# Reads of repeated a and b over all SBUF ports, v in six DMAs, and another order of the first interleaved batch, in a polysketch attention with a sinkhorn-routed MoE behind it

## The chip, the core and the metric

The kernel runs on one core of a Trainium2 chip. The metric is the device time of one execution in microseconds. TensorE (PE) does the matrix products, VectorE (DVE) and ScalarE (ACT) the elementwise work, GpSimd (POOL) some sums and weights, and SyncE (SP) issues nearly all DMA transfers. On-chip memory (SBUF) has 128 partitions; PSUM is the memory into which TensorE writes. All data are float32.

## The reference

Sizes: B = 4 batches, H = 4 heads, S = 1088 positions, D = 32 per head, r = 8 sketch rows; then N = 4352 tokens of 128 numbers, E = 8 experts of F = 1024 hidden units.

```
def phi(x):                                   # 64 features from two sketches of 8
    a = einsum('rd,bhsd->bhsr', S1, x)
    b = einsum('rd,bhsd->bhsr', S2, x)
    return einsum('bhsi,bhsj->bhsij', a, b).reshape(..., 64)
kv  = einsum('bhsf,bhsd->bhfd', phi(k), v);   z = sum(phi(k), axis=2)
num = einsum('bhsf,bhfd->bhsd', phi(q), kv)
den = einsum('bhsf,bhf->bhs', phi(q), z)[..., None] + 1e-06
x   = (num / den) transposed to (B*S, H*D) = (4352, 128)

P = exp(x @ w_gate - max)                     # 4352 x 8
for _ in range(8):
    P /= P.sum(1, keepdims=True) + 1e-09;  P /= P.sum(0, keepdims=True) + 1e-09;  P *= N / E
out = sum over e of P[:, e:e+1] * (relu(x @ w1[e]) @ w2[e])
```

So every token goes through every expert, and P is only a weight. That is why experts 0 and 1 can be computed before P is known (their results are weighted later), and why the big products can start while most of the attention is still to be done.

## The kernel before

**The big products.** Nearly all TensorE time is in the MoE: `first` (L895) multiplies w1 by columns of x into a PSUM bank, ScalarE applies relu (L899), VectorE forms sums and differences of blocks (L912 for the form with seven products, L957 for that with twenty), and `second`/`into` (L1068) multiplies w2, or sums of its blocks, by these into the banks s. The generator `steps()` yields one step of this at a time: one first product and the second products that fall due, 8 steps behind (`LAG`). `fill(n)` takes steps from it until n units are done; a unit is 480 columns. The first groups of columns belong to experts 0 and 1 without weights: 2 x 256 and 2 x 288 columns of batch 0 for expert 0, 2 x 256 for expert 1, then three times 2 x 480 and 2 x 192 columns of batches 1 to 3. After routing, weighted columns xe = xT * P (L664 on GpSimd) of the other experts follow to the end.

**The attention.** Batch 0 is written out by hand at the start, before any step of the MoE can run; its last third, `multiply(2)`, `fractions(2)`, `divide(2)`, falls after the first `fill`. Batches 1 to 3 are interleaved with the MoE. Their parts:

- `transpose_k` (L293, VectorE) turns k, `keys_ab` (L299, TensorE, matmuls at L306 and L310) makes the two sketches of the keys, `keys_products` (VectorE) their outer products, `keys_sums` (L328, TensorE) kv and z together, with a slot of ones beside the heads' slots of v giving z; `keys_kept` (L344) copies the result from PSUM to kvs.
- `transpose_q` (L290) turns q; `queries_ab` (L417, matmuls at L426) makes the sketches a and b of the queries, ScalarE copies them from PSUM to the tile qab, and SyncE writes them to DRAM (qa, qb). Some are written several times over: the outer product of a and b needs each a beside each b on 64 partitions per pair of heads.
- `repeat` (L438) reads them back repeated: rb from qb in two DMAs of 64 partitions, and ph from qa in eight DMAs, each to the partitions j, j+8, j+16 and so on.
- `times` (L449) multiplies ph by rb on VectorE, a third of the positions at a time; `tops` (L453, TensorE, L460) multiplies by kvs; `over` (L470, VectorE) divides; `take_over` (L481) writes the turned result to DRAM (xd) and reads it into xT in four DMAs. From xT the MoE takes its columns.

`attention(b)` (L497) strings these together with the next batch's keys and queries in between: at its first points come `keys_sums(b)`, `times(b,0)`, `transpose_q(b+1)`, then `keys_kept(b)`, `queries_ab(b+1)`, `times(b,1)`, `tops(b,0)`, then `times(b,2)`, `repeat(b+1)`, `over(b,0)`, `tops(b,1)`. Between any two points 1.4 units of MoE work are filled in. `routing` follows with 5 units before its first product and 3.75 per iteration of P; then its result goes through DRAM (pT) to the weighted columns.

**What sets the order.** In these stretches the order of instructions on TensorE and VectorE is that of the program text (`tc.manual_schedule`), so a waiting instruction holds up everything behind it on its engine. ScalarE's relus and the DMA issues on SyncE's one queue are placed by the scheduler, in practice close to the order of the text. Four PSUM banks serve all first products and the small products of attention in turn (`bank()`).

**Buffers.** ph has two buffers (one batch each, by turns), rb, qT, kT, qab, kp have one, v two, q two, k one. So `repeat(b+1)` can read rb only when the last `times(b,2)` is done, and `load_k(b+2)` can start only when `transpose_k(b+1)` is done.

## Time and profile before

Device time: 950.99 us, the median of 3 runs (949.77 to 951.51). The profiled execution has a span of 949.6 us.

| stretch of the span, us | TensorE busy, us | granted TensorE clock | DMA share | what happens |
|---|---|---|---|---|
| 0 to 20 | 16.92 | 1.00 | 0.63 | batch 0 of attention by hand, with 15 products at the start that only keep TensorE busy |
| 20 to 50 | 19.18 | 0.87 | 0.80 | end of batch 0, keys and queries of batch 1, first MoE steps |
| 50 to 110 | 55.52 | 0.95 | 0.80 | batches 1 to 3 between MoE steps |
| 110 to 200 | 86.64 | 0.98 | 0.10 | plain experts 0 and 1; the end of attention and routing |
| 200 to 215 | 15.00 | 1.00 | 0.27 | the first weighted columns are made |
| 215 to 950 | 726.81 | 1.00 | 0.44 | weighted experts |

The sizes of the transfers in question, and their median time from issue to landing: qb from qab 576 KB, 5.7 us (two a batch); qa from qab 72 KB, 5.7 us (two); rb from qb 576 KB, 5.6 us (two); ph from qa 144 KB, 7.5 us (eight); k and q 544 KB, 5.6 and 7.1 us; v 64 KB, 3.3 us (eight a batch) and 8 KB, 3.1 us (four).

How to read it: "busy" is the time in which an engine executes, without its waits. The granted clock is the share of full speed that TensorE was given[...]. The DMA share is the mean busy share of the core's 16 DMA engines. A line such as "PE a L426 <- DVE qT L291" in a view of waits says that TensorE's instruction at line 426, which writes tile a, waited for VectorE's instruction at line 291 that writes qT. In the chain of the end, each line is a start time, a duration and what ran or was waited for, and "DMA rb<-qb" is a transfer into rb from qb.

### The profile page before, as it was taken

What the parts mean: (1) busy time and instruction counts of PE and PEld (TensorE: products, weight loads), DVE (VectorE), ACT (ScalarE), POOL (GpSimd) and SP (SyncE); (2) the same over time, 40 slices, a digit from 0 to 9 for tenths busy, and PEclk for the clock granted to TensorE, in tenths of its full rate; (3) what the DMA queues carried; (4) which work ended last, traced back from release to release, by engine and by line L of the source; (5) the groups of instructions that cost most, each with busy time, mean ns of one, the idle gap of its engine ahead of it and who ended that gap; (6) DMA issues with size and microseconds to landing.
All of it is one profiled execution on the core that took longest, in us unless ns stands there. A gap on an engine that the chain in (4) does not pass through costs nothing.

```text
span 949.6 us, 18935 instructions
## 1 busy us (share of the span) xinstructions
PE 920.1 (97%) x7434; PEld 554.6 (58%) x7434; DVE 692.8 (73%) x1204; ACT 417.8 (44%) x905; POOL 195.3 (21%) x182
## 2 busy tenths in 40 slices
PE   8789899999999999999999999999999999999997
PEld 5567544556666666665555555555555555556964
DVE  7479669878678779567786665976666977778655
ACT  2334344555444445444544444544444544445443
POOL 2010000026357611031010200120111333320210
PEclk9889999999999999999999999999999999999999
DMA  5977610023243354553544353445343455552640
GB/s 168 234 198 199 150 47 1 1 85 128 95 139 123 106 191 138 155 177 107 163 128 147 124 166 113 145 122 167 128 145 109 148 189 175 161 186 89 170 148 12
DMA packets 93928, 127.70 MB, mean 134 GB/s; under 512 B 25904, under 2 KB 71984, under 8 KB 89488
## 3 DMA queue, kind: packets, MB, share of 16 engines
q1 hardware_dynamic: 92608, 126.34, 43.8%
q8 instruction: 58, 0.95, 0.4%
q10 hardware_dynamic: 1232, 0.16, 0.1%
q14 instruction: 30, 0.25, 0.1%
HBM read 107.88 MB, written 18.60 MB: 133 GB/s over the span
## 4 chain that ended last, share of the span: by engine, by line
PE 86%; DVE 6%; DMA 5%; issue 1%; ACT 1%; SPq 1%; POOL 0%; DVEq 0%; ACTq 0%
PE a L895 45%; PE s L1068 39%; DMA rb<-qb 2%; DMA qx<-in_q_dram 1%; DVE hb L912 1%; DMA w<-in_moe_w_dram 1%; DMA qb<-qab 1%; PE a L460 1%; DVE hb L957 1%; DMA xd<-xt 0%; PE a L426 0%; DVE pqg L957 0%; PE a L337 0%; DVE kept L721 0%; DVE cs L594 0%
## 5 line engine op out<-in xcount | busy, mean ns | idle before, releaser
L895 PE MATMUL a<-xe,w 128*64 128x256 f32 (+1 forms) x2560 | 518.2, 470 | 0.0
L899 ACT ACTIVATE hb<-a 128x256 f32<-128x256 f32 (+5 forms) x408 | 195.2, 480 | 260.5 <-PE a L895 235.1
L899 ACT ACTIVATE hx<-a 128x256 f32<-128x256 f32 (+1 forms) x360 | 167.4, 465 | 214.2 <-PE a L895 193.0
L895 PEld LDWEIGHTS a<-xe,w 128*64 128x64 f32 x2560 | 207.7, 137 | 79.3 <-issue 2.2
L1068 PE MATMUL s<-hb,ws 128*64 128x256 f32 (+4 forms) x1344 | 239.1, 395 | 2.1 <-DVE hb L912 1.6
L1068 PE MATMUL s<-hx,ws 128*64 128x256 f32 x1280 | 204.8, 379 | 0.4 <-DVE kept L724 0.4
L957 DVE TENSOR_TENSOR hx<-hx 128x512 f32<-128x512 f32 (+1 forms) x204 | 151.7, 753 | 70.1 <-ACT hx L899 65.0
L957 DVE TENSOR_TENSOR hb<-hb 128x512 f32<-128x512 f32 (+1 forms) x204 | 133.4, 665 | 94.3 <-ACT hb L899 90.3
L664 POOL TENSOR_TENSOR xe<-xT,xe 128x768 f32<-128x768 f32 (+2 forms) x41 | 84.1, 2053 | 563.7 <-DMA xe<-pT 545.8
L1068 PEld LDWEIGHTS s<-hb,ws 128*64 128x64 f32 x1344 | 113.9, 137 | 111.5 <-issue 82.3
L1068 PEld LDWEIGHTS s<-hx,ws 128*64 128x64 f32 x1280 | 106.3, 137 | 98.6 <-issue 74.3
L895 PE MATMUL a<-xT,w 128*64 128x480 f32 (+4 forms) x512 | 123.0, 475 | 1.0 <-DVE xT L410 0.9
L1068 PE MATMUL s<-hb,w 128*64 128x256 f32 (+4 forms) x496 | 102.1, 412 | 1.8 <-DVE kept L724 1.8
L912 DVE TENSOR_TENSOR hb<-hb 128x480 f32<-128x480 f32 (+8 forms) x96 | 64.5, 673 | 20.6 <-ACT hb L899 11.0
L1068 PE MATMUL s<-hx,w 128*64 128x256 f32 x384 | 68.3, 379 | 0.0
L895 PEld LDWEIGHTS a<-xT,w 128*64 128x64 f32 x512 | 51.3, 141 | 28.3 <-issue 17.6
L241 POOL TENSOR_TENSOR ws<-w 128x256 f32<-128x256 f32 (+1 forms) x70 | 59.8, 890 | 14.1 <-PE a L895 10.6
L1068 PEld LDWEIGHTS s<-hb,w 128*64 128x64 f32 x496 | 45.4, 138 | 27.9 <-issue 10.9
L912 DVE TENSOR_TENSOR hx<-hx 128x256 f32<-128x256 f32 (+1 forms) x65 | 38.7, 600 | 25.0 <-ACT hx L899 23.9
L957 DVE TENSOR_TENSOR pqg<-hb 128x512 f32<-128x512 f32 x68 | 48.3, 750 | 0.0
L1068 PEld LDWEIGHTS s<-hx,w 128*64 128x64 f32 x384 | 34.2, 137 | 10.6 <-DVE hx L912 0.3
L957 DVE TENSOR_TENSOR pqg<-hx 128x512 f32<-128x512 f32 x68 | 35.8, 566 | 0.0
(164 smaller groups left out, 468.9 us busy)
## 6 DMA issues: line engine op xcount, KB each, us to landing
w<-in_moe_w_dram SPq DMA_DIRECT2D x82, 512.0 KB, 5.4
ws<-ws SPq DMA_DIRECT2D x34, 1024.0 KB, 5.0
xe<-pT SPq DMA_DIRECT2D x34, 384.0 KB, 4.3
ws<-ws SPq DMA_DIRECT2D x12, 512.0 KB, 4.4
qb<-qab SPq DMA_DIRECT2D x6, 576.0 KB, 5.7
rb<-qb SPq DMA_DIRECT2D x6, 576.0 KB, 5.6
ph<-qa SPq DMA_DIRECT2D x24, 144.0 KB, 7.5
pb<-pT SPq DMA_DIRECT2D x6, 384.0 KB, 7.4
```

What stands on the lines that cost most here:

```text
L241: tc.keep_in_program_order(nc.gpsimd.tensor_tensor(ws[:, c:c + len(ns)], blocks(x), blocks(y), op=Alu.subtract if off else Alu.add))
L460: nc.tensor.matmul(pn[64 * s:64 * (s + 1), t, 2 * i:2 * i + 2].rearrange("p h d -> p (h d)"), ph[:, i, s, 64 * t:64 * (t + 1)], kvs[b % 2] ...
L664: tc.keep_in_program_order(nc.gpsimd.tensor_tensor(out, x, pb, op=Alu.mult))
L895: nc.tensor.matmul(ph[sl], loaded_w[j][0][:, P * f + H2 * s:P * f + H2 * (s + 1)], sources[j][:, lo:hi], start=True, stop=True, tile_posit ...
L899: nc.scalar.activation(out=out, in_=ph, func=Act.Relu)
L912: nc.vector.tensor_tensor(out, a, b, op=Alu.subtract)
L957: nc.vector.tensor_tensor(out if not isinstance(out, tuple) else places(*out), places(*a), places(*b) if isinstance(b, tuple) else b, op=A ...
L1068: nc.tensor.matmul(sums[g][i][H2 * s:H2 * (s + 1), n * place:n * (place + 1)], w, x, start=c == 1, stop=c == per, tile_position=(0, H2 * s))
```

## The change

It has four parts. First, the way in which a and b of the queries are stored in DRAM and read back. a is now stored twice (one write of 144 KB per half instead of 72 KB), so that ph can be read in four DMAs of 288 KB, each to the partitions j, j+4, j+8 and so on. b is stored by parity of the head in the pair, in four writes of 288 KB, so that rb can be read in one DMA over all 128 partitions. [...] `repeat` is split into `repeat_a`, which stands directly behind the writes in `attention`, and `repeat_b`, which stays where `repeat` was because rb has one buffer; the writes of a now go ahead of those of b.

Second, v is loaded for all four heads at once, in six DMAs per batch for twelve. For that the slot of ones moves from the middle of the tile v to its end, the slots that `keys_sums` multiplies follow, and `keys_kept` and `fractions` use the changed order of kv and z; `keys_kept` is one copy per engine instead of two.

Third, the order of batch 1's beginning: `multiply(2)` and `fractions(2)` of batch 0 come ahead of `transpose_q(1)`, and the loads of k, q and v of batch 2 stand behind `transpose_k(1)`, ahead of `keys_ab(1)`.

Fourth, more MoE steps stand between these parts: 11 units from the first `fill` to `attention(1)`, where there were 8.5.

```
--- before.py
+++ after.py
@@ -151,7 +151,7 @@
     v_slots = []
     for i in range(2):
         t = wk.tile([P, H + 1, NT + 1, D], F32, name=f"v{i}", bufs=1)
-        nc.vector.memset(t[:, 2], 1.0)
+        nc.vector.memset(t[:, H], 1.0)
         v_slots.append(t)
 
     loaded, pools = {}, []
@@ -167,18 +167,15 @@
         loaded["q", b] = qx
 
     def load_v(b):
-        vx = v_slots[b % 2]
-        for p in range(2):
-            o = v[b, 2 * p].offset
-            slots = slice(3 * p, 3 * p + 2)
-            for c in range(4):
-                nc.sync.dma_start(
-                    out=vx[32 * c:32 * (c + 1), slots, 0:NT, :].rearrange("p h t d -> p h (t d)"),
-                    in_=AP(tensor=v.tensor, offset=o + NT * D * c, ap=[[SA * D, 32], [S * D, 2], [1, NT * D]]))
-            for c in range(2):
-                nc.sync.dma_start(
-                    out=vx[32 * c:32 * (c + 1), slots, NT, :],
-                    in_=AP(tensor=v.tensor, offset=o + (4 * NT + c) * D, ap=[[SA * D, 32], [S * D, 2], [1, D]]))
+        vx, o = v_slots[b % 2], v[b].offset
+        for c in range(4):
+            nc.sync.dma_start(
+                out=vx[32 * c:32 * (c + 1), 0:H, 0:NT, :].rearrange("p h t d -> p h (t d)"),
+                in_=AP(tensor=v.tensor, offset=o + NT * D * c, ap=[[SA * D, 32], [S * D, H], [1, NT * D]]))
+        for c in range(2):
+            nc.sync.dma_start(
+                out=vx[32 * c:32 * (c + 1), 0:H, NT, :],
+                in_=AP(tensor=v.tensor, offset=o + (4 * NT + c) * D, ap=[[SA * D, 32], [S * D, H], [1, D]]))
 
     load_k(0)
     load_q(0)
@@ -328,7 +325,8 @@
 
         kp, vx = products.pop(b), v_slots[b % 2]
         pv = bank()[:, 0:128].rearrange("p (i c d) -> p i c d", i=2, c=2)
-        slots = (slice(0, 3, 2), slice(1, 3), slice(2, 4), slice(2, 5, 2))
+
+        slots = [slice(h, H + 1, H - h) for h in range(H)]
 
         for t in range(NT + 1):
             n = P if t < NT else 64
@@ -343,22 +341,16 @@
 
     def keys_kept(b):
         pv = sums_of.pop(b)
-
-        f = pv.rearrange("p i c d -> p (i c d)")
         for s in range(2):
             sl = slice(64 * s, 64 * (s + 1))
-            for i in range(2):
-                if not b:
-                    x, y = kvz[sl, :, i, s, :], pv[sl, i]
-                elif i:
-                    x, y = kvs[b % 2][sl, :, s, D], f[sl, 2 * D - 1:2 * D + 1]
-                else:
-                    x = kvs[b % 2][sl, :, s, 0:D]
-                    y = AP(tensor=f.tensor, offset=f[sl].offset, ap=[f[sl].ap[0], [3 * D, 2], [1, D]])
-                if s:
-                    nc.vector.tensor_copy(x, y)
-                else:
-                    nc.scalar.copy(x, y)
+            if b:
+                x, y = kvs[b % 2][sl, :, s, :], pv[sl].rearrange("p i c d -> p i (c d)")[:, :, 0:D + 1]
+            else:
+                x, y = kvz[sl, :, :, s, :], pv[sl].rearrange("p i c d -> p c i d")
+            if s:
+                nc.vector.tensor_copy(x, y)
+            else:
+                nc.scalar.copy(x, y)
 
     chunks = ((0, 384), (384, 736), (736, S))
 
@@ -388,7 +380,7 @@
         pn, pd = bank(), bank()
         for t, m in ((pd, 1), (pn, 0)):
             for i in range(2):
-                nc.tensor.matmul(t[64 * i:64 * (i + 1), 0:n], kvz[:, (i + m) % 2, i].rearrange("p h d -> p (h d)"),
+                nc.tensor.matmul(t[64 * i:64 * (i + 1), 0:n], kvz[:, m, i].rearrange("p h d -> p (h d)"),
                                  phs[0][:, i, lo:hi], start=True, stop=True, tile_position=(0, 64 * i))
         queries[0, c] = pn, pd
 
@@ -415,8 +407,8 @@
 
 
     def queries_ab(b):
-        qa = dram.tile([H * R, 2, 2 * W9], F32, name=f"qa{b}")
-        qb = dram.tile([R, R * H, 2, 2 * W9], F32, name=f"qb{b}")
+        qa = dram.tile([H * R, 2, 2, 2 * W9], F32, name=f"qa{b}")
+        qb = dram.tile([2, R, 2 * R, 2, 2 * W9], F32, name=f"qb{b}")
         ab = wk.tile([P, 3, 192], F32, tag="qab", name="qab", bufs=1)
         x = qT.rearrange("p (h q c t s) -> p h c t q s", h=2, q=2, c=3, t=3)
         for cs in ((0, 1), (2,)):
@@ -429,19 +421,20 @@
             nc.scalar.copy(ab[:, cs[0]:cs[-1] + 1], pq)
         abf = ab.rearrange("p c n -> p (c n)")
         for s in range(2):
-            nc.sync.dma_start(out=qb.rearrange("i f s n -> s f i n")[s],
-                              in_=abf[64 * s + 32:64 * (s + 1)].unsqueeze(1).to_broadcast([32, R, 2 * W9]))
+            x = abf[64 * s:64 * s + 32].unsqueeze(1).to_broadcast([32, 2, 2 * W9])
+            nc.sync.dma_start(out=qa[:, :, s], in_=x)
         for s in range(2):
-            nc.sync.dma_start(out=qa[:, s], in_=abf[64 * s:64 * s + 32])
+            for h in range(2):
+                x = abf[64 * s + 32 + h:64 * (s + 1):2].unsqueeze(1).to_broadcast([2 * R, R, 2 * W9])
+                nc.sync.dma_start(out=qb[h, :, :, s].rearrange("i f n -> f i n"), in_=x)
         queries[b] = qa, qb
 
-    def repeat(b):
-        qa, qb = queries.pop(b)
-        for h in range(2):
-            nc.sync.dma_start(out=rb[64 * h:64 * (h + 1)],
-                              in_=qb.rearrange("i (j x h) s n -> h (i j) x (s n)", x=2, h=2)[h])
-        for j in range(R):
-            nc.sync.dma_start(out=phs[b % 2][j::R], in_=qa.rearrange("(x r) s n -> r x (s n)", x=2))
+    def repeat_a(b):
+        for j in range(4):
+            nc.sync.dma_start(out=phs[b % 2][j::4], in_=queries[b][0].rearrange("(x r) j s n -> (r j) x (s n)", x=2))
+
+    def repeat_b(b):
+        nc.sync.dma_start(out=rb, in_=queries.pop(b)[1].rearrange("h i (j x) s n -> (h i j) x (s n)", x=2))
 
     def third(t, c):
         return t.rearrange("p i (s c n) -> p i s c n", s=2, c=3)[:, :, :, c]
@@ -514,12 +507,13 @@
         keys_kept(b)
         if follows:
             queries_ab(b + 1)
+            repeat_a(b + 1)
         times(b, 1)
         tops(b, 0)
         yield
         times(b, 2)
         if follows:
-            repeat(b + 1)
+            repeat_b(b + 1)
         over(b, 0)
         tops(b, 1)
         yield
@@ -1161,19 +1155,23 @@
         divide(1)
     with tc.manual_schedule(engines={engines.DVE, engines.PE}):
         fill(1)
-        transpose_q(1)
-        queries_ab(1)
-        repeat(1)
         multiply(2)
         fractions(2)
         fill(1)
+        transpose_q(1)
+        queries_ab(1)
+        repeat_a(1)
+        repeat_b(1)
+        fill(1)
+        divide(2)
+        fill(1)
         transpose_k(1)
-        divide(2)
-        keys_ab(1)
         load_k(2)
         load_q(2)
         load_v(2)
-        fill(2)
+        fill(1)
+        keys_ab(1)
+        fill(1.5)
         keys_products(1, 0)
         fill(1.5)
         keys_products(1, 1)
```

## The prediction

> **What bounds the kernel now.** I read the page first: its engine rows, then its clock row. TensorE is busy 920.1 of 949.6 us, so at most 29.5 us of idle time, plus what a lowered clock costs, can be won without taking work away.

> ```profile
> PE 920.1 (97%) x7434; PEld 554.6 (58%) x7434; DVE 692.8 (73%) x1204; ACT 417.8 (44%) x905; POOL 195.3 (21%) x182
> PEclk9889999999999999999999999999999999999999
> ```

> The second view is TensorE's own waits, longest first (total, times, longest). Nearly half of the idle time is three single waits:

> ```profile
> PE a L426 <- DVE qT L291: 6.5, 1, 6.5
> PE a L460 <- DVE kvs L359: 4.1, 1, 4.1
> PE a L306 <- DVE kT L297: 3.3, 1, 3.3
> ```

> The third is the chain of the end between 0 and 120 us, which says what stood behind each of them:

> ```profile
> 31.48 8.03 DMA rb<-qb
> 39.53 0.53 SPq L444
> ...
> 40.74 8.05 DMA qx<-in_q_dram
> ...
> 48.81 1.32 DVE qT L291
> ...
> 50.27 2.19 PE a L426 x12
> ...
> 93.90 8.00 DMA rb<-qb
> 101.92 0.53 SPq L444
> ```

> The reader is to see that all three end in transfers. Gap 1 (25.2 to 28.5): VectorE waits for k of batch 1. Gap 2 (43.8 to 50.3): VectorE stands at times(1,0) until 45.6 because the last ph read left the queue at 39.5; q of batch 2 was queued behind those reads, at 40.74, and landed at 48.8. Gap 3 (106.4 to 110.5): times(3,0) waits until 107.0 for the reads of batch 3 (101.4 is when VectorE was free).

> The fourth view is a table of 2-us windows (PE, weight load, DVE, ACT, POOL busy; clock; DMA share; GB/s):

> ```profile
> 36.00:38.00 2.00, 2.00 (x22) 1.58 (x20) 1.62 (x4) 0.85 (x3) 0.00 (x0) 1.00 1.03 210
> 44.00:46.00 2.00, 0.00 (x0) 0.00 (x0) 0.40 (x1) 0.00 (x0) 0.00 (x0) 0.95 1.00 381
> 50.00:52.00 2.00, 1.73 (x12) 1.41 (x12) 1.87 (x7) 0.14 (x1) 0.00 (x0) 0.50 0.36 88
> 74.00:76.00 2.00, 2.00 (x21) 1.36 (x18) 1.93 (x6) 0.93 (x3) 0.00 (x0) 1.00 1.01 370
> 100.00:102.00 2.00, 2.00 (x42) 1.53 (x40) 1.39 (x4) 1.65 (x5) 0.00 (x0) 1.00 1.07 207
> ```

> While rb and ph are read (34 to 44, 64 to 72, 96 to 106) all 16 DMA engines are occupied but move only 203 to 236 GB/s; loads of k and q over all partitions run at 370 to 381. And after a gap the clock is 0.50.

> [...]

> **The change, part by part.** The order of instructions is fixed by the build, so I follow it with durations of the trace.

> *Reads.* Per batch 8 x 144 + 2 x 576 KB = 2.36 MB. At 215 GB/s that is 11.0 us. The new ph reads go to every fourth partition and rb is one transfer over 128[...], 6.3 at the trace's 375. I take 300 GB/s, 7.9 us[...]; bounds 6.3 and 11.0. Bytes written are nearly unchanged (qa doubles, +144 KB). SyncE issues five reads for ten, at 0.59 us each 3 us less.

> *v in six DMAs for twelve:* in front of k of batch 1 stand twelve issues fewer; these and their waits held k back from 12.2 to 22.6. k and q of batch 2 now go before the repeats and should be in by about 23.

> *Order of batch 1.* multiply(2) comes first, so qT is turned by 22.7 (21.8 before), the a/b products end near 24.8 and ScalarE's copies near 25.2, against 23.55. In exchange TensorE has five steps (0.43 us of first products each, 0.22 of second in all) ahead of keys_ab, which fill gap 1. The new limit is VectorE: one block's sums (1.6) when ScalarE has its fourth block at 24.2, divide(2) (2.2, 28.39 to 30.58 in the trace), transpose_k (1.4): keys_ab near 29.25, TensorE out of work near 27.4. So a wait of 1.85 stays. keys_ab is 0.8 later than at 28.48 but 2.4 us of work are done: +1.6. The half clock of 28.8 to 32 cost 1.6 (0.69 and 0.50 of two windows); I count it as won: **3.2**, bounds 1.6 (the clock still falls) and 5.3 (no wait).

> *Gap 2.* The writes (1.44 MB) start at 25.3; before, 1.84 MB with k took 7.2 us, so they land near 31.5. [...]rb is issued at 31.5, all data by 39.4; at 215, by 42.5. VectorE wants them at 38.2 (its fourth block's sums need TensorE's step 15, near 35.8). times(1,0) 0.95 and qT 1.3 end at 41.7; TensorE comes to the a/b products of batch 2, five steps later in its order than before, at 44.5. The q load is long there. So 6.5 us go, and the half clock from 50.27 to 56.0, worth 2.9. Behind the waiting VectorE lie the next block's sums, needed near 45.5, and kvs: 0.5 lost. **8.9**, bounds 5.6 (slow reads, 3.8 lost) and 9.4.

> *Gap 3.* From the a/b products of batch 3 (81.41) to the data took 25.5 us. Now: copies +1.9, first a write, the four xT reads, then b, landed at +10.4; reads done at +19 (at 215, +22). VectorE wants them at about +20, TensorE's tops(3,0) at +25. Gap 3 and its half clock (110.5 to 114, 1.6) go: **5.7**, lower bound 4.

> *A new wait.* take_over(1)'s reads into xT are issued behind the write of a for batch 3, which waits for ScalarE's copy. Before, the products that use them (first 128x480, 91.30) came 9.9 us after the a/b products; in the new order two tops and three steps lie between, 1.0 + 0.8 + 2.4 + 0.8 = 5.0. Copy +1.9, a write 0.4, four issues of 0.43, landing 3.0 after the last (the view of xT: 3.0 to 6.1): +6.7. **-1.7**, bounds 0 and -5.

> *VectorE* is 93 to 97% busy from 56 to 100 us, and TensorE's gaps let it catch up: **-1.0**, bounds 0 and -3. keys_kept in one copy per engine for two saves 0.15 us of VectorE a batch: nothing, beside TensorE work. The startup up to 20 us is VectorE's own chain: nothing.

> *Later.* Two and a half units more of fill push routing's last product from 190.1 to about 194.4 in today's time; qT then comes some 3 us later than 195.2. xe (202.45) stands behind w2, which waits for TensorE until 201.8, and the first weighted product (212.87) comes 4.0 after GpSimd's (208.9): nothing.

> Sum: 3.2 + 8.9 + 5.7 - 1.7 - 1.0 = 15.1; 951.0 - 15.1 = **935.9 us**.

> **Rivals.** *Reads stay at 215 GB/s* (a small source read again and again could bind elsewhere): gap 2 gives 5.6, gap 3 about 3.7, so 9.8 in all: 941.2. For it: nothing in the trace shows a strided partition read at 300.[...] *Everything clears*: 5.3 + 9.4 + 5.7 = 20.4: 930.6. For it: TensorE waited only 0.6 us between 56 and 104. Against: the xT order. *The new xT wait takes gap 3's place*: 5 us, a half clock again (1.7), VectorE -2: 15.1 - 5.0 - 1.0 - 1.0 = 8.1, so about 943. For it: landings up to 6.1. Against: the small a write in front, where 576 KB of b stood. *Slower*: the xT wait as above, no gain at gap 1 (-3.2), and routing so late that the weighted stage waits: 943 + 3 + about 7 = 953. Against it: 4 us of slack there, and that the long waits lie in one place.

> **How the numbers follow.** Forecast 0.47; slow reads 0.17; everything clears 0.18; xT 0.10; slower 0.05; gains and losses cancel 0.03. The range, 929.5 to 944.0, holds the first four, with the bounds of the parts. Faster 0.92, same 0.03, slower 0.05.

> **What would show it.** Reads of rb and ph at about 300 GB/s and over; no wait of L426 on qT, none of the tops on kvs; a wait near 1.9 us at keys_ab and one of 1 to 3 us of the first 128x480 products on xT; clock 1.00 from 30 us on. It is wrong if the windows of the reads stay near 215, if the clock falls after the keys_ab wait, if TensorE waits for VectorE in small pieces from 45 to 110, or if xe arrives after the first weighted product wants it.

## The result, and the profile after

The changed kernel takes 938.89 us (median of 4 runs, 937.17 to 941.17) where the kernel before, on the same chip, takes 950.50 (949.77 to 951.51): a ratio of 0.9879, 95% interval 0.9855 to 0.9903, 11.6 us less. The forecast was 935.9, range 929.5 to 944.0. The profiled execution is the fastest of the four, with a span of 935.3 us against 949.6. The profiled execution of the kernel before took 951.57 us, longer than any of its four here, so the two profiles lie 14.3 us apart where the medians lie 11.6.

The page of the changed kernel, its engine row, its clock row and the shares of the chain that ended last:

```profile
PE 914.8 (98%) x7434; PEld 556.6 (60%) x7434; DVE 696.3 (74%) x1200; ACT 416.6 (45%) x901; POOL 195.9 (21%) x182
...
PEclk9999999999999999999999999999999999999999
...
PE 90%; DVE 8%; issue 1%; ACT 1%; POOL 0%; DVEq 0%; ACTq 0%; POOLq 0%
```

Of the 14.3 us between the two spans, 9.0 are idle time of TensorE (29.5 before, 935.3 - 914.8 = 20.5 after), and 5.3 are busy time for the same 7434 products. The parts that count are 8.1 and 6.2: the products at the start that only keep TensorE busy are booked 0.97 us longer (6.42 for 5.45) in place of a wait of 0.88, and the first real product starts at 7.3 us in both. The busy part is the clock, which cost 1.6, 2.9 and 1.6 us behind the three gaps before: from 20 to 120 us its mean is 1.00 for 0.91, and no stretch is at 0.50 now. What 0.50 means for a product is in the trace of the kernel before: 128x480 products take 1.02 us on the mean from 110.7 to 114.0, at 0.50, and 0.57 us from 120 to 130, at 1.00. And no transfer is left in the chain of the end, where transfers had 5%.

TensorE's waits after the change (between 18 and 125 us: total, times, longest), where 6.5, 4.1 and 3.3 us stood:

```profile
PE a L889 <- DVE hb L906: 2.5, 1, 2.5
PE a L303 <- DVE kT L294: 2.3, 2, 1.4
PE a L453 <- ACT qab L421: 1.3, 1, 1.3
PE a L418 <- ACT f L736: 1.2, 1, 1.2
PE a L889 <- DVE xT L402: 0.9, 1, 0.9
```

In order of time they are: 0.89 us at keys_ab of batch 1 (28.4 us), 1.25 us and 1.30 us around the a/b products of batch 2 (45 to 49 us), 1.4 us at keys_ab of batch 2 (59.8), and 2.55 us at the first products of 480 columns (81.2 to 83.7). The names in the second column mislead in two places. Where "ACT f L736" is named, VectorE ends qT at 46.02, 0.15 us before TensorE goes on. And the first product of 480 columns doesn't wait for hb: in run e6 below it starts before the same instruction on hb. It was the four xT reads, the last of which was issued at 80.2 and took 3.3 us.

The windows of the changed kernel while a and b are written and read, where the kernel before showed 203 to 229 GB/s in the windows of its reads (34 to 44, 64 to 72, 96 to 106) and, after its gaps, a clock of 0.50:

```profile
26.00:28.00 2.00, 1.95 (x19) 1.06 (x16) 1.79 (x6) 1.53 (x4) 0.00 (x0) 1.00 0.38 82
28.00:30.00 2.00, 1.11 (x29) 0.77 (x27) 1.97 (x4) 0.38 (x1) 0.00 (x0) 1.00 0.83 179
30.00:32.00 2.00, 2.00 (x33) 1.87 (x30) 1.63 (x3) 1.12 (x4) 0.00 (x0) 1.00 0.98 188
32.00:34.00 2.00, 2.00 (x22) 1.85 (x19) 1.06 (x3) 1.00 (x3) 0.00 (x0) 1.00 1.01 251
...
36.00:38.00 2.00, 2.00 (x21) 1.72 (x19) 1.31 (x3) 1.17 (x3) 0.00 (x0) 1.00 0.94 339
38.00:40.00 2.00, 2.00 (x29) 1.61 (x27) 0.56 (x2) 0.86 (x3) 0.00 (x0) 1.00 1.00 361
...
44.00:46.00 2.00, 0.92 (x9) 0.29 (x4) 2.00 (x3) 1.97 (x6) 0.00 (x0) 1.00 1.09 219
```

The reader is to see two things. While the reads run (36 to 40), the engines move 340 to 360 GB/s. But the writes before them run at 82 to 188 until 32, and so rb still comes too late for VectorE, which stands at times(1,0), on VectorE's own list of work:

```profile
38.15 0.41 DVE L319 TENSOR_TENSOR kp<-ab 64x256 f32<-64x256 f32 x1
43.84 0.96 DVE L444 TENSOR_TENSOR ph<-ph,rb 128x768 f32<-128x768 f32 x1 [5.28 <-DMA rb<-qb]
44.72 1.30 DVE L288 STREAM_TRANSPOSE qT<-qx 128x1088 f32<-128x1088 f32 x1
```

### The profile page after: what moved, and what is told of

Its sections match the earlier page's. It is cut to its first block, busy times and chain, and to the rows that moved or that the text cites. A ratio compares the mean times of both kernels' runs of the same rounds, so it can differ in the third digit from the quotient of the medians.

```text
span 935.3 us, 18858 instructions
## 1 busy us (share of the span) xinstructions
PE 914.8 (98%) x7434; PEld 556.6 (60%) x7434; DVE 696.3 (74%) x1200; ACT 416.6 (45%) x901; POOL 195.9 (21%) x182
## 3 DMA queue, kind: packets, MB, share of 16 engines
q1 hardware_dynamic: 91888, 126.78, 43.8%
## 4 chain that ended last, share of the span: by engine, by line
PE 90%; DVE 8%; issue 1%; ACT 1%; POOL 0%; DVEq 0%; ACTq 0%; POOLq 0%
PE a L889 47%; PE s L1062 40%; DVE hb L906 2%; PE a L335 1%; PE a L114 1%; PE a L303 0%; PE a L453 0%; DVE rs L582 0%; DVE ph L444 0%; DVE p L585 0%; DVE cs L588 0%; DVE kp L319 0%; DVE kept L715 0%; DVE w L718 0%; DVE kT L292 0%
## 5 line engine op out<-in xcount | busy, mean ns | idle before, releaser
L889 PE MATMUL a<-xT,w 128*64 128x480 f32 (+4 forms) x512 | 119.4, 463 | 3.7 <-DVE hb L906 2.5
L906 DVE TENSOR_TENSOR hx<-hx 128x256 f32<-128x256 f32 (+1 forms) x65 | 39.1, 607 | 24.5 <-ACT hx L893 23.4
L951 DVE TENSOR_TENSOR pqg<-hb 128x512 f32<-128x512 f32 x68 | 48.8, 759 | 0.0
L951 DVE TENSOR_TENSOR pqg<-hx 128x512 f32<-128x512 f32 x68 | 35.8, 566 | 0.0
```

The lines of the kernel that those rows point to most:

```text
L889: nc.tensor.matmul(ph[sl], loaded_w[j][0][:, P * f + H2 * s:P * f + H2 * (s + 1)], sources[j][:, lo:hi], start=True, stop=True, tile_posit ...
L906: nc.vector.tensor_tensor(out, a, b, op=Alu.subtract)
L951: nc.vector.tensor_tensor(out if not isinstance(out, tuple) else places(*out), places(*a), places(*b) if isinstance(b, tuple) else b, op=A ...
```

## The experiments

Each run has 4 executions, beside 7 of the kernel before. Ratios are to the kernel before on the same chip. "All ports" is the author's name, in the title and the recorded texts, for reads to all 128 partitions or to every fourth, and "half of the ports" for reads to 64 neighbouring partitions or to every eighth. No trace shows ports; e1 and e2 measure how fast reads to these partitions go.

**e1, reads to 64 partitions and to every eighth.** The changed kernel with each read put back to the partitions it went to before the change (the code is shortened here and in e6 and e7):

```
-    for j in range(4):
-        sync.dma_start(out=ph[j::4], in_=qa "(r j) x (s n)")
+    for j in range(R):
+        sync.dma_start(out=ph[j::R], in_=qa[:, j // 4] "r x (s n)")
-    sync.dma_start(out=rb, in_=qb "(h i j) x (s n)")
+    for h in range(2):
+        sync.dma_start(out=rb[64 * h:64 * (h + 1)], in_=qb[h])
```

> The changed kernel, with the same bytes stored in the same four and two writes and read at the same places[...]: ph in eight transfers to every eighth partition, rb in two of 64 partitions. If the ports set the rate, as I predicted, the windows of the reads fall from about 340 to about 215 GB/s, rb of batch 1 lands 3 to 5 us after the 43.8 us of the changed kernel, and all of that reaches the end, because VectorE is busy without a break from there to 84 us: 942 to 945 us. If the gain came from the order of the work alone and the reads' rate is hidden, the time stays within 1 us of 938.9.

Measured: 943.70 us, ratio 0.9913 (0.9885 to 0.9942). The windows of this run while it reads:

```profile
36.00:38.00 2.00, 2.00 (x22) 1.72 (x19) 1.60 (x4) 1.12 (x3) 0.00 (x0) 1.00 0.94 220
38.00:40.00 2.00, 2.00 (x37) 1.66 (x35) 0.27 (x1) 0.82 (x2) 0.00 (x0) 1.00 0.87 166
40.00:42.00 2.00, 2.00 (x59) 1.77 (x55) 0.00 (x0) 0.17 (x1) 0.00 (x0) 1.00 0.99 244
42.00:44.00 2.00, 2.00 (x20) 1.25 (x18) 0.00 (x0) 1.57 (x6) 0.00 (x0) 1.00 1.02 226
```

The DMA engines are nearly as busy as in the changed kernel, but move half to three quarters as much from 36 to 42. VectorE gets rb at 47.1 us for 43.8, TensorE waits 4.8 us for qT, and its clock is 0.50 from 48.7 to 55.5 us. There are ten reads for five here, though, so e1 alone can't tell the partitions from the number of issues.

**e2, ten reads to 128 partitions and to every fourth.** Each read of the changed kernel split into halves of a row (`ph[j::4, x]` and `rb[:, x]`, x = 0, 1), so that there are ten again.

> The changed kernel, with ten reads a batch as before the change[...]: ph in eight transfers (every fourth partition, one half of the row each), rb in two (all 128 partitions, one half of the row each). If the ports count, the reads keep about 340 GB/s and the time stays within 1.5 us of 938.9, the more so since the first reads run while the later ones are issued. If it is the number of issues on SyncE (five more at 0.6 to 0.9 us) that counts, it is as slow as the run with half of the ports, 942 to 945 us.

Measured: 939.38 us, ratio 0.9878 (0.9848 to 0.9908), rb at 43.6. On the same chip e1 takes 4.3 us more with as many issues: the partitions that a read goes to count, and the number of issues is not the cause. The windows of e2:

```profile
36.00:38.00 2.00, 2.00 (x20) 1.75 (x18) 1.48 (x4) 1.21 (x3) 0.00 (x0) 1.00 0.79 239
38.00:40.00 2.00, 2.00 (x34) 1.62 (x31) 0.39 (x2) 0.82 (x2) 0.00 (x0) 1.00 0.78 173
40.00:42.00 2.00, 2.00 (x61) 1.83 (x57) 0.00 (x0) 0.06 (x1) 0.00 (x0) 1.00 0.99 396
42.00:44.00 2.00, 2.00 (x20) 1.25 (x18) 0.36 (x1) 1.57 (x5) 0.00 (x0) 1.00 1.02 415
```

They show where the partitions tell. From 36 to 40, while ten reads are issued one after the other, e2 moves hardly more than e1, but with engines that are only 0.78 to 0.79 busy; so the expected 340 GB/s are missed there. From 40 to 44 the engines are full in both, and e2 moves 396 to 415 GB/s where e1 moves 226 to 244. In all, the packets of ph and rb take 9.5 us in e2 and 9.0 in the changed kernel (34.0 to 43.1), and 12.2 in e1.

The trace of this run also shows something on the clock. The wait for xT is 2.2 us here, and behind it the clock is down:

```profile
82.00:84.00 2.00, 0.78 (x4) 0.40 (x6) 1.93 (x5) 0.00 (x0) 0.00 (x0) 0.99 0.89 241
84.00:86.00 2.00, 2.00 (x10) 1.14 (x8) 0.85 (x2) 0.57 (x1) 0.00 (x0) 0.50 0.99 233
86.00:88.00 2.00, 2.00 (x11) 1.03 (x10) 0.00 (x0) 0.57 (x1) 0.00 (x0) 0.65 0.93 228
```

That is 1.0 + 0.7 = 1.7 us. In the profile of the changed kernel the clock stays at 1.00 after a wait of 2.55 us; the last section shows how the two differ.

**e3, the old order.** The changed kernel with batch 1's beginning as before the change (`transpose_q(1)`, the a/b products and the reads first; `load_k(2)`, `load_q(2)`, `load_v(2)` behind `keys_ab(1)`; 8.5 units).

> The changed kernel with the beginning of batch 1 in the order of the kernel before, and its 8.5 units of filling work. By my prediction's steps the order is worth the 3.2 us of gap 1, and q of batch 2 falls back behind the reads of rb, so that a wait of some 4 us on qT comes back near 42 us, with a lowered clock: 943 to 947 us. If the reads alone made the gain, it stays within 1 us of 938.9; the xT reads would then still be waited for.

Measured: 941.92 us, ratio 0.9898 (0.9873 to 0.9923). Its TensorE waits between 18 and 125 us:

```profile
PE a L418 <- DVE qT L288: 8.2, 2, 7.6
PE a L453 <- issue: 1.1, 1, 1.1
```

The wait on qT is nearly twice what I expected. q of batch 2 is queued behind rb again, as expected, and is turned at 45.3 us; but TensorE is out of work at 39.2 us already, because gap 1 is not there (in e5 below, where it stays, at 42.6). Yet the run is better than expected, because neither the wait for xT nor one on kT is there: with 2.5 units less ahead of the attention, the products of 480 columns come later beside it. So the new order is worth some 2 to 3 us beside e2, e4 and the changed kernel, with intervals that overlap, and it brings the wait for xT with it.

**e4, v in twelve loads.** The changed kernel with two heads per load of v.

> The changed kernel with v loaded in twelve transfers a batch for six (two heads each), the slot of ones at the end as in the changed kernel. My theory: k of batch 1 and q of batch 2 are issued 3 us later, at about 16.5 and 18.7 us, which is still long before the 27.9 us at which VectorE turns k; v of batch 2 is needed only at 71 us. So within 1 us of 938.9. The rival, that fewer v transfers freed the queue where it counted: 2 to 4 us slower.

Measured: 939.49 us, ratio 0.9876 (0.9850 to 0.9901). In the new order the six loads are worth nothing that shows, as expected, but not for the reason given: k of batch 1 is issued at 23.4 us for the 16.5 expected (13.3 in the changed kernel), and is still there in time for VectorE, which turns it at 27.9 as in the changed kernel. In the old order they do matter, as e5 shows.

**e5, the reads alone.** The kernel before with the new storing and reading of a and b in the old places.

> The kernel before with the first part of the change alone: a stored twice, b in four writes, ph read in four transfers and rb in one, all at the places of the kernel before; v in twelve loads, the old order. If the reads' rate is worth something by itself: gap 3 (4.1 us and 1.6 of lowered clock) goes, gap 2 shrinks by 2 to 3 us since q of batch 2 still stands behind the reads, gap 1 stays: 943 to 946 us. If the reads help only together with the new order: within 1 us of 950.5.

Measured: 941.58 us, ratio 0.9904 (0.9868 to 0.9941): 9.5 us of the 11.6, more than I gave it. Its two longest waits of TensorE:

```profile
PE a L426 <- DVE qT L291: 3.4, 1, 3.4
PE a L306 <- DVE kT L297: 2.5, 1, 2.5
```

Gap 3 is gone. Gap 1 (2.5 us, and a clock of 0.50 after it) stays: VectorE waits 3.7 us for k, which stands behind twelve loads of v. In e3, with the same order of batch 1 and six loads, k is turned at 22.5 us for 26.2 and gap 1 is gone. So either the six loads or the new order takes gap 1 away. In e3 it comes back as a longer gap 2 (7.6 us), and the two runs take the same time.

**e6, the xT reads first.** On the changed kernel:

```
+    ordered = tc.keep_in_program_order
-    nc.sync.dma_start(out=xd, ...)          # and the four reads into xT
+    ordered(nc.sync.dma_start(out=xd, ...))
-    nc.sync.dma_start(out=qa[...], ...)     # and the writes of qb
+    ordered(nc.sync.dma_start(out=qa[...], ...))
```

> The changed kernel, with the reads of batch 1's result into xT kept ahead of the writes of a and b of batch 3 on SyncE's queue. In the changed kernel TensorE waits 2.55 us at 83.7 us before the first products of 480 columns; the profile names a VectorE instruction, I take it for these reads. If I am right the wait goes; VectorE then becomes the next limit, since it is busy without a break up to 84.9 us, so that 1 to 2.5 us are won: 936.5 to 938. If it is VectorE that is waited for, as the profile says, the wait stays and the time is the same, 938.9.

Measured: 935.38 us (933.31 to 935.59), ratio 0.9829 (0.9813 to 0.9845). In the changed kernel SyncE holds the xT reads until ScalarE's copy for qa is done, here not. The first view is SyncE's work in the changed kernel. The second is TensorE's waits between 18 and 125 us in this run:

```profile
67.72 0.34 SPq L477 DMA_DIRECT2D xd<-xt  x1
77.52 0.60 SPq L425 DMA_DIRECT2D qa<-qab  x1
78.23 2.41 SPq L479 DMA_DIRECT2D xT<-xd  x4
80.68 0.59 SPq L425 DMA_DIRECT2D qa<-qab  x1
```

```profile
PE a L303 <- DVE kT L294: 2.7, 2, 1.8
PE a L455 <- ACT qab L423: 1.3, 1, 1.3
PE a L420 <- DVE qT L288: 0.9, 1, 0.9
```

The largest wait is gone, though VectorE does the same work in the same order, and TensorE's first product of 480 columns starts 2 us before the instruction on hb that the profile of the changed kernel named:

```profile
80.65 0.60 PE L891 MATMUL a<-xT,w 128*64 128x480 f32 x1
82.63 0.84 DVE L908 TENSOR_TENSOR hb<-hb 128x256 f32<-128x256 f32 x2
```

So it was the reads. The gain of 3.5 us between the medians is more than the wait of 2.55. The two profiled executions, neither of which is at half clock here, lie 3.8 us apart; what makes up the rest is not shown. Other executions of the changed kernel may lose another 1.7 us to the clock behind the wait, as e2 does; their traces aren't there.

**e7, b stored once.** To take the slow writes away, b was written in two writes of 72 KB and read repeated:

```
+    x = qb[h] "j (x s n)", repeated R times in front
+    sync.dma_start(out=rb[64 * h:64 * (h + 1)], in_=x)      # h = 0, 1
```

> The changed kernel, with b stored once in two writes of 72 KB for four of 288 KB, and rb read repeated from it in two transfers of 64 partitions[...]. ph as in the changed kernel. My reading of the changed kernel is that the four writes of b, at about 188 GB/s and 3.6 us of issue, made rb 4 us later than predicted. If so, rb of batch 1 lands at 39 to 41 us for 43.8 although it is read at about 215 GB/s, the two waits of 1.25 and 1.3 us at 45 to 49 us go, and VectorE is 3 to 4 us earlier: 933 to 936 us. If half of the ports cost more than the writes save: 939 to 942.

**e8** is e7 with the xT reads first.

> The last two edits together: b stored once[...], and the reads into xT ahead of the writes of batch 3. If both causes are real and lie at different times, the gains add: 931 to 935 us. If VectorE bounds the stretch from 44 to 85 us anyway, no better than the better one of the two alone.

Measured: 943.77 us, ratio 0.9922 (0.9901 to 0.9943), and 942.33, ratio 0.9905 (0.9882 to 0.9927). Both miss. The writes are short now (rb is issued from 31.8 us on), but rb comes at 48.7 us. The windows of e7 show less than the rate of e1's reads:

```profile
42.00:44.00 2.00, 2.00 (x22) 1.29 (x20) 0.00 (x0) 1.36 (x5) 0.00 (x0) 1.00 0.51 95
44.00:46.00 2.00, 1.01 (x10) 0.35 (x6) 0.00 (x0) 1.97 (x6) 0.00 (x0) 1.00 0.48 124
```

In e1, whose reads of rb go to 64 partitions as well, the engines are busy (a DMA share of 0.87 to 1.02) at 166 to 244 GB/s. Here the share is 0.48 to 0.51, at 95 to 124 GB/s. These reads repeat b R = 8 times in front. Whether that leaves the engines idle is not shown, since another form of the same read was not tried. In e8 the wait for xT is there too (1.8 us), since all of batch 1 comes later behind the slow reads of b: its result is written at 80.1 us, 67.7 in the changed kernel. So these two runs don't test what the writes cost.

**e9 and e10, more steps ahead of attention(1).** On e6, the last `fill(1.5)` before the attention of batch 1 becomes `fill(3.5)` and `fill(4.5)`.

> The run with the xT reads first, and two more units of MoE steps (3.5 for 1.5) between the last keys' products of batch 1 and its attention. My theory of the waits left at 44 to 48 us (0.9 and 1.3) is that VectorE stands at times(1,0) from 38 to 43 us for a late rb, with sums that TensorE soon needs queued behind it. Two units give it those sums ahead of the wait, and TensorE 1.7 us of work: both waits go, and some of the 1.8 us on kT at 61 us: 932 to 934 us for 935.4. The first weighted products had 3.6 us to spare. If VectorE's total work is the bound from 44 to 85 us, whatever the order: 935 to 936.

> The same with three more units. If rb's lateness is covered by two, a third gains nothing (within 1 us of the run with two); if it isn't, another 0.5 to 1 us. A unit too many would push routing against the weighted stage, whose first products have about 3.6 us to spare, less 2.6: slower by up to 1 us.

Measured: 936.74 us, ratio 0.9851 (0.9827 to 0.9875), and 937.67, ratio 0.9859 (0.9837 to 0.9880). The waits of e9 between 18 and 125 us:

```profile
PE a L891 <- DMA xT<-xd: 3.9, 1, 3.9
PE a L303 <- DVE kT L294: 0.9, 1, 0.9
```

The waits at 44 to 49 us and on kT of batch 2 are gone, as my theory of them says. But the time is not won: the wait for xT is back, 3.9 us in e9 and 6.3 in e10, and behind it comes the half clock (0.50 from 78.8 to 82.2 us in e9). As I read these two runs, what bounds the stretch is the stock of steps on batch 0, which are all that TensorE can do until the first result of batch 1 is in xT. Steps that are taken early to cover one wait are missing at the next.

**e11, the order without the reads.** The changed kernel with a and b stored and read as before the change.

> The changed kernel with the whole first part undone: a and b stored as before the change (a once, b in two writes), ph read in eight transfers and rb in two[...]. What is left is v in six loads and the new order of batch 1. If the gains of reads and order add (9.5 for the reads alone, 12.1 for both), it takes 2 to 4 us off the kernel before: 947 to 949. If they overlap, because both take away the same gap 2, it is 943 to 945, like the changed kernel with half of the ports.

Measured: 945.35 us, ratio 0.9941 (0.9918 to 0.9964): 5.2 us less than before. Reads alone give 9.5, order and v 5.2, together 11.6, not 14.7. By the intervals (5.6 to 12.6, 3.4 to 7.8 and 9.2 to 13.8) an overlap of 3 us is not clear of noise, but the traces show that there is one: gap 3 is gone in both e5 and e11. In e11 a wait of 3.8 us for xT stands in its place, with 6.8 us of half clock behind it. e11 has the two old writes of b, and its windows while it writes are:

```profile
28.00:30.00 2.00, 1.12 (x34) 0.92 (x32) 1.97 (x4) 0.23 (x1) 0.00 (x0) 1.00 0.99 236
30.00:32.00 2.00, 2.00 (x29) 1.87 (x27) 1.63 (x3) 1.28 (x4) 0.00 (x0) 1.00 0.93 233
```

That looks faster than the 179 to 188 GB/s of the four writes from 16 partitions in the changed kernel. But it is no price of the two kinds of write: in the same windows the same four writes show 204 and 202 in e1 and 169 and 222 in e2, and between 26 and 28 us e11's writes show 182. What writing b from 16 partitions instead of 32 costs, no run shows.

**e12, what stands behind rb.** On e6, `load_q(2)` and `load_v(2)` ahead of batch 1's first `fill`.

> The run with the xT reads first, with v of batch 2 loaded together with q of batch 2, at about 16 us, ahead of all writes. Behind rb of batch 1 in SyncE's queue stand then k (544 KB) and the two weight loads of expert 1 (1 MB), which no longer have to wait for rb, where k and v (1.1 MB in all) stood. My prediction held that what is issued behind a read doesn't slow it. By the bytes of the changed kernel's trace some 0.8 MB of k and v moved before rb had landed. If transfers behind rb share the engines with it, rb lands 1 to 2 us after the 43.2 of the run before, and the time is 935 to 938 us. If they don't, rb lands at 43.2 or before: 933 to 935.5.

Measured: 934.39 us (933.90 to 936.19), ratio 0.9826 (0.9804 to 0.9847), which is the same as e6 within the intervals. VectorE gets rb at 43.4 us, 43.2 in e6, with 0.5 MB more behind it. So here more loads behind this read don't hold it up, as was assumed. The load of k stands directly behind rb in both runs, and what that one costs is not tested.

## Why the prediction was right, and where it was off

The direction, the place and most of the size were right: three long waits for transfers went, with the half clock behind them. e1 and e2 show that the rate of the reads was the cause it was taken for, and e3 that the order adds something, 2 to 3 us with intervals that overlap. Step by step, in the profiled executions:

| step | predicted, us | measured, us | how |
|---|---|---|---|
| gap 1 | +3.2 | +3.8 | 3.3 and 1.6 of clock before; 0.89 and a short wait of 0.24 (at 25.3 us) after |
| gap 2 | +8.9 | +6.9 | 6.5 and 2.9 of clock before; 1.25 + 1.30 after |
| gap 3 | +5.7 | +5.7 | 4.1 and 1.6 of clock before; nothing after |
| new wait on xT | -1.7 | -2.55 | the wait at 81.2 us |
| VectorE | -1.0 | -1.4 | kT of batch 2 late at 59.8 us |
| sum | 15.1 | 12.45 | |

The remaining 1.9 of 14.3 us are a wait of 0.66 on the first a/b products that the order took away, and small ones. The later stages give nothing, as said: the first weighted product comes at 199.2 us for 212.9, so 13.7 us are won by then. That the sum comes so close in the profile (14.3 for 15.1) is in part luck: gap 2, xT and VectorE were together 3.25 us too good, and 0.6 in gap 1 and the 1.9 that were not counted made up for most of it.

**The term that was off in gap 2** is "The writes (1.44 MB) start at 25.3; before, 1.84 MB with k took 7.2 us, so they land near 31.5". I took 255 GB/s from a stretch in which a fast load of k was counted in. The windows from 26 to 34 us sum to 2 x (82 + 179 + 188 + 251) = 1400 KB, so that the 1.47 MB of writes end near 34.3, 2.8 us later. In the first of them the DMA share is only 0.38: the two writes of a take 2.21 us to issue, and the first write of b is issued at 27.75. The reads then take 9.5 us until 43.84, 248 GB/s for their own 2.36 MB, where I took 300, an estimate between the 215 of the old reads and the 375 of the loads of k and q: another 1.6. In the windows from 36 to 40, which they fill alone, they do run at 339 to 361; the time goes at their end, where k and v move beside the last of rb, which itself is out by 43.1. Together 4.4, and 39.4 + 4.4 is the 43.8 measured. It is worked out from bytes; what the writes cost by themselves no run shows, since e7 failed to take them away. e9 fits that the two waits left in gap 2 come from this lateness: with more work in front of it they go.

**The wait on xT** was rightly foreseen with its cause (e6), and 0.85 us too short. The four reads took 2.41 us to issue for 4 x 0.43 = 1.72, and the terms written down (1.9, 0.4, 1.72 and 3.0) add up to 7.0 and not to 6.7.

**The half clock** comes well before such a gap ends. In the trace of the kernel before it falls to 0.50 at 45.82, only 2.05 us after TensorE ran out of work at 43.77; the last section has the working. The 1.7 us of the rival on xT is the author's estimate; behind gap 3 the clock was 0.50 for 3.41 us (110.67 to 114.09), half of which is 1.7. And the 203 to 236 GB/s given for the old reads are 203 to 229 in the windows named.

**Between profile and median** lies the rest. The profiled execution of the changed kernel is 1.7 us below its median, that of the kernel before 1.1 above. The other three executions of the changed kernel, 1.3 to 4.0 us longer than the profiled one, have mean clocks of 0.997, 0.997 and 0.993 for 0.998. My forecast had a clock of 1.00 from 30 us on. e2 and e4 show the half clock after this very wait; the traces of the other three executions aren't there, so that for them it is an inference.

**The rivals.** "Reads stay at 215 GB/s" is ruled out: e1 builds that world and takes 943.70 us (the rival said 941.2), 4.3 more than e2 on the same chip. "Everything clears" fell on gap 2 and xT. "The xT wait takes gap 3's place" has the right wait and half its size (and one of its two terms of 1.0 has no source); e11, without the new reads, comes nearer to it. "Slower" and "cancel" found nothing in the trace.

## What to carry to other kernels

Reads into half of the partitions, or into every eighth, kept the DMA engines busy here at little more than half the rate (226 to 244 GB/s for the halves in e1 and 194 to 221 for both kinds in e11, 396 to 415 in e2), so look at GB/s beside the DMA share. Where loads wait in one in-order queue, one write that waits for a copy held back reads that could go 7 us earlier (71.0 us in e6 for 78.2): keep the ready ones in front (e6, the best of this study with e12 at 935.4 and 934.4 us). And when filling work is moved ahead to cover a wait, ask what it was covering where it stood (e9).

## What the runs showed of the hardware that was not expected

```profile
80.57:83.98 3.41, 1.26 (x21) 0.81 (x17) 3.31 (x8) 0.00 (x0) 0.00 (x0) 1.00 0.91 252
83.98:87.39 3.41, 3.41 (x14) 1.82 (x12) 0.87 (x2) 1.02 (x2) 0.00 (x0) 0.50 0.99 233
```

```profile
78.59:82.00 3.41, 2.59 (x44) 2.32 (x40) 3.27 (x7) 0.97 (x3) 0.00 (x0) 1.00 0.79 191
82.00:85.41 3.41, 1.68 (x11) 0.93 (x13) 2.90 (x6) 0.57 (x1) 0.00 (x0) 1.00 1.01 235
```

In e2 TensorE is idle for 2.15 us of one window, and the next is at half clock. In the changed kernel the longer wait is split by the edge at 82.00, 22 windows behind the first record of its clock at 6.91: 0.82 us lie before it and 1.73 behind, and the clock stays at 1.00. As I read it, that is luck of where the edges lay. The other traces agree. Up to 200 us, each of the 17 windows at full clock with 2.03 us or more of idle time is followed by half clock (in the kernel before 3.15, 2.05 and 3.25 us), and none of those with 1.80 or less (in the changed kernel 1.75 at most). From half clock, TensorE came back behind windows with 0.66 us or less idle, and stayed down behind those with 0.71 or more (in the kernel before it stayed down behind 1.04 us from 49.23 to 52.65, and came back behind the window from 52.65 to 56.06 without idle time). So a window needn't be idle throughout: 2.05 of 3.41 us, 60%, was enough. The exact limits are not shown, only these two sides of them.
